# ssm_k loaded and transposed in two halves of its channels, three stage 1 copies moved from VectorE to ScalarE, and the last copies of two stages halved

## The chip, the cores and the metric

The kernel runs on one core of one Trainium2 chip. The metric is the device time of one execution in microseconds (us), the lower the better; a kernel's figure is the median of its runs. "Same" means within 2%. Even fast runs of one kernel on one chip differ by up to 2.9 us here (224.88 to 227.79 us, at mean granted TensorE clocks of 0.999 and 0.985 of full speed), so stages are compared by the trace and not by the total alone.

## The reference, cut to what matters

```python
x = A_q                                            # 1 x 2048 x 512, bf16
# kv = (4-tap causal filter of k with shift_k) * v, per channel
kv_f = rfft(pad(kv));  kf_f = rfft(pad(ssm_k))     # ssm_k: 512 channels x 2048 times
y = irfft(kv_f * kf_f)[:2048] + kv * ssm_D         # long convolution, per channel
h = x + layernorm(x) * y
out = h + relu(layernorm(h) @ w1) @ w2
```

The long convolution is done with matmuls: a transform of ssm_k in two stages, the same for kv, a product, and two inverse stages. Then comes the MLP. ssm_k is stored with time as the last axis, but the first stage needs channels and coarse time on the rows; so the kernel transposes it on TensorE as soon as it is loaded.

## The kernel before

ssm_k is loaded at once (2 MB) as `sk` with 128 partitions, 4 channel blocks and 2048 times. Each of 64 transposes takes every 64th time of all four blocks: 128 weight columns (4 blocks x 32 times), 64 elements apart in memory. Eight share a PSUM bank, which VectorE or ScalarE then copies out.

```python
sk = early.tile([P, DC, S], BF16, name="sk")
nc.sync.dma_start(out=sk[:], in_=A_ssm_k.rearrange("(c p) t -> p c t", p=P))
...
def to_rows(src, q, fl, eng):
    pst = psum.tile([P, 8, P], BF16, tag="ps", name="pst")
    for i in range(8):
        nc.tensor.transpose(out=pst[:, i, :], in_=src[:, :, :, 8 * q + i], identity=ident[:])
    copy(eng, fl[:, :, :, 8 * q:8 * q + 8], pst[:].rearrange("p i (d g) -> p g d i", d=2))
...
skv = sk[:].rearrange("p c (a b) -> p c a b", b=64)
for q in range(8):
    to_rows(skv, q, kfl, "DADADADA"[q])
...
taps(0)                       # 4 matmuls of 512 columns: the filter of k
for gb in range(7):
    group_k(gb)               # stage 1 of ssm_k: 64 loads and 64 matmuls in 0.6 us, 4 copies
    taps(2 * gb + 1)
    taps(2 * gb + 2)
taps(15)
group_k(7)
# then xfl: 64 transposes of kv; the spectrum stage; the product stage, whose end is
#   finish(): psy -> kf   copy("AD"[s] if kp >= 14 else "A", kf[:, s, :, ...], psy)
# then inverse stage 1, b = 0..31 (psi -> bp); the second inverse (pz) needs all of bp
    if b < 31:
        copy("ADAADAAD"[b % 8], dst, ps[:])
    else:
        copy("A", dst[:, 0], ps[:, 0])
        copy("D", dst[:, 1], ps[:, 1])
    ...
    if b in (19, 22, 25, 28):
        row_stats(mv1, (b - 19) // 3)      # VectorE
```

## Time and profile before

| what | before |
|---|---|
| time, median of 3 | 223.93 us (223.79 to 223.94) |
| span of the profiled run | 221.4 us, clock 0.999 |
| sk released | 9.73 us |
| the 64 transposes of sk | 9.73 to 16.07 |
| first stage 1 group, with one tap done | 17.16 |
| transposes of kv start (xfl) | 37.48 |
| product starts | 66.82 |
| inverse stage 1 starts | 98.44 |
| second inverse starts | 114.97 |

The last seven rows are read from the chain of waits and from TensorE's timeline. TensorE is in 85% of that chain, so one can take the kernel as a row of stages on TensorE and ask of each part of the change whether its stage begins or ends sooner. The view of one tile tells how a group of instructions repeats. For `sk` of the kernel before (columns: line, engine, operation, count, shortest/median/longest duration in ns, first and last start in us, shapes):

```profile
L203 PEld LDWEIGHTS <-sk x64: 167/190/212, 9.7 to 15.7; 128*128 128x128 bf16 x64
L203 PE MATMUL pst<-ident,sk x64: 224/258/349, 9.7 to 15.8; 128*128 128x128 bf16 x64
```

The duration of one (258 ns) is not its cost, since they are pipelined. The cost is the distance of starts: (15.8 - 9.7) / 63 = 97 ns on average, cold start included. ("Cold" is the slow clock with which the array begins: in this trace the starts are about 107 ns apart until 12.8 us, and about 88 ns after it, when the array is "warm". The clock column of the views shows 1.00 in both parts.)

### The profile page before, as it was taken

What the parts mean: (1) busy time and instruction counts of PE and PEld (TensorE: products, weight loads), DVE (VectorE), ACT (ScalarE), POOL (GpSimd) and SP (SyncE); (2) the same over time, 40 slices, a digit from 0 to 9 for tenths busy, and PEclk for the clock granted to TensorE, in tenths of its full rate; (3) what the DMA queues carried; (4) which work ended last, traced back from release to release, by engine and by line L of the source; (5) the groups of instructions that cost most, each with busy time, mean ns of one, the idle gap of its engine ahead of it and who ended that gap; (6) DMA issues with size and microseconds to landing.
All of it is one profiled execution on the core that took longest, in us unless ns stands there. A gap on an engine that the chain in (4) does not pass through costs nothing.

```text
span 221.4 us, 7288 instructions
## 1 busy us (share of the span) xinstructions
PE 201.6 (91%) x3111; PEld 140.1 (63%) x3111; DVE 150.3 (68%) x299; ACT 133.0 (60%) x252; POOL 72.0 (33%) x103
## 2 busy tenths in 40 slices
PE   0299799999989999989989899999999999999993
PEld 0294446999978999969977578544444444444452
DVE  4898788889997999966878779761973257130031
ACT  2868877888885888867983889103650066206500
POOL 8399940000008999978400120220022002000000
PEclk9999999999999999999999999999999999999999
DMA  5999920000000000019990000152113110421012
GB/s 178 311 223 204 193 53 4 0 4 6 3 3 3 1 0 0 4 47 238 258 340 14 3 3 3 24 82 58 31 28 80 42 48 4 95 56 42 0 43 54
DMA packets 30384, 15.41 MB, mean 70 GB/s; under 512 B 25520, under 2 KB 29072, under 8 KB 30224
## 3 DMA queue, kind: packets, MB, share of 16 engines
q1 hardware_dynamic: 29520, 14.76, 29.0%
q8 instruction: 24, 0.39, 0.7%
q10 hardware_dynamic: 832, 0.20, 0.4%
q14 instruction: 8, 0.07, 0.1%
HBM read 7.08 MB, written 2.10 MB: 41 GB/s over the span
## 4 chain that ended last, share of the span: by engine, by line
PE 85%; ACT 5%; DMA 4%; DVE 2%; issue 1%; SPq 0%; DVEq 0%; ACTq 0%
PE ps2m L536 18%; PE ps1m L524 16%; PE pz L450 8%; PE psy L343 7%; PE psi L417 7%; PE pkv L262 6%; PE pst L203 6%; PE ps L221 4%; PE ps2k L236 4%; DMA sk<-in_A_ssm_k_dram 4%; PE ps2k L238 3%; PE u L236 3%; PE u L238 3%; ACT ecore L131 1%; ACT zt L461 1%
## 5 line engine op out<-in xcount | busy, mean ns | idle before, releaser
L526 ACT ACTIVATE h1T<-ps1m 128x512 bf16<-128x512 f32 (+3 forms) x55 | 27.4, 514 | 21.2 <-PE ps1m L524 20.3
L524 PE MATMUL ps1m<-hlnT,w 128*128 128x512 bf16 (+3 forms) x220 | 39.6, 336 | 0.3
L536 PE MATMUL ps2m<-w,h1T 128*128 128x512 bf16 (+3 forms) x187 | 39.8, 367 | 0.0
L538 DVE TENSOR_TENSOR o<-ps2m,xh 128x512 bf16<-128x512 f32 (+1 forms) x17 | 11.1, 659 | 37.6 <-PE ps2m L536 32.2
L524 PEld LDWEIGHTS <-w 128*128 128x128 bf16 (+1 forms) x220 | 21.7, 100 | 17.6 <-issue 1.4
L536 PEld LDWEIGHTS <-h1T 128*128 128x128 bf16 (+1 forms) x187 | 17.6, 98 | 21.2 <-issue 3.1
L333 DVE TENSOR_TENSOR t<-u,kf 128x704 fp32r<-128x704 f32 x32 | 26.7, 883 | 3.0 <-ACT usb L329 2.8
L333 POOL TENSOR_TENSOR t<-usb,kf 128x320 fp32r<-128x320 f32 x32 | 28.2, 935 | 1.4 <-ACT usb L329 1.0
L461 ACT CAST zt<-pz 128x512 bf16<-128x512 f32 x16 | 8.4, 593 | 29.5 <-PE pz L450 29.5
L450 PE MATMUL pz<-bp,ecore 32*32 32x128 f32 x1024 | 23.1, 384 | 1.7 <-DVE bp L210 0.9
L470 POOL TENSOR_SCALAR rstd<-mv 128x4 f32<-128x4 f32 (+1 forms) x7 | 1.6, 232 | 70.1 <-DVE mv L477 70.1
L208 ACT CAST a<-ps 128x512 fp32r<-128x512 f32 (+1 forms) x38 | 19.3, 568 | 4.3 <-PE ps L221 4.3
L450 PEld LDWEIGHTS pz<-bp,ecore 32*32 32x32 f32 x1024 | 14.4, 103 | 9.1 <-issue 5.0
L210 DVE CAST a<-ps 128x512 fp32r<-128x512 f32 (+1 forms) x30 | 18.5, 651 | 2.2 <-PE ps L221 2.1
L208 ACT CAST kf<-psy 128x512 fp32r<-128x512 f32 x30 | 17.4, 641 | 1.8 <-PE psy L343 0.3
L475 DVE BATCH_NORM_STATS2 st<-xh 128x6 f32<-128x512 bf16 x28 | 17.3, 678 | 0.0
L262 PE MATMUL pkv<-kT,wdiag 128*128 128x512 bf16 x64 | 15.4, 380 | 1.2 <-issue 1.2
L417 PE MATMUL psi<-dre,kf 128*128 128x256 f32 x64 | 15.5, 284 | 0.9 <-DVE kf L210 0.9
L343 PE MATMUL psy<-t,ipos 128*128 128x512 f32 x48 | 15.9, 391 | 0.0
L417 PE MATMUL psi<-dim,kf 128*128 128x256 f32 x64 | 15.4, 283 | 0.0
L203 PE MATMUL pst<-ident,sk 128*128 128x128 bf16 x64 | 6.3, 277 | 9.7 <-DMA sk<-in_A_ssm_k_dram 9.7
L265 DVE TENSOR_TENSOR vT<-pkv,vT 128x512 bf16<-128x512 f32 x16 | 10.9, 691 | 3.4 <-PE pkv L262 3.4
(113 smaller groups left out, 394.9 us busy)
## 6 DMA issues: line engine op xcount, KB each, us to landing
sk<-in_A_ssm_k_dram SPq DMA_DIRECT2D x1, 2048.0 KB, 8.4
out_dram<-o SPq DMA_DIRECT2D x58, 32.0 KB, 1.6
xh<-in_A_q_dram SPq DMA_DIRECT2D x4, 384.0 KB, 6.8
w<-in_B_w_dram SPq DMA_DIRECT2D x1, 1376.0 KB, 12.8
w<-in_B_w_dram SPq DMA_DIRECT2D x1, 1280.0 KB, 16.2
xh<-in_A_q_dram SPq DMA_DIRECT2D x4, 128.0 KB, 2.8
hlnT<-hln SPq DMA_TRANSPOSE x12, 2.4
w<-in_B_w_dram SPq DMA_DIRECT2D x1, 96.0 KB, 15.9
```

The lines of the kernel that those rows point to most:

```text
L203: nc.tensor.transpose(out=pst[:, i, :], in_=src[:, :, :, 8 * q + i], identity=ident[:])
L208: nc.scalar.copy(out=o, in_=i)
L210: nc.vector.tensor_copy(out=o, in_=i)
L262: nc.tensor.matmul(out=ps[:], lhsT=wdiag[:, rg, j, :], rhs=kT[:, rg, CH * c + 16 - j:CH * c + CH + 16 - j], start=(j == 0), stop=(j == KS ...
L333: eng.tensor_tensor(out=t[:, :, j, :], in0=in0.unsqueeze(1).to_broadcast([P, 2, n, 2]), in1=kfr[:, :, j, ks], op=ALU.mult)
L343: nc.tensor.matmul(out=psy[:], lhsT=m_[:], rhs=t_.rearrange("p j k -> p (j k)"), start=first, stop=not first)
L417: nc.tensor.matmul(out=ps[:, i, :], lhsT=kf[:, c, 4 * m:4 * m + 4, :].rearrange("p r k -> p (r k)"), rhs=d[:].rearrange("p a b -> p (a b)" ...
L450: nc.tensor.matmul(out=pz[32 * a:32 * a + 32, r4, l4, :], lhsT=ecore[rows, rho, n2, :], rhs=rhs, start=(rho == 0), stop=(rho == 1), tile_p ...
L475: nc.vector.bn_stats(out=st[:, t % 4, :], in_=xh[:, t, :])
L524: nc.tensor.matmul(out=ps1[:fsz, :], lhsT=w1[:, c, fc * P:fc * P + fsz], rhs=hlnTs[sc][:, c, part], start=(c == 0), stop=(c == DC - 1))
L526: nc.scalar.activation(out=h1s[sc][:fsz, fc, part], in_=ps1[:fsz, :], func=ACT.Relu)
L536: nc.tensor.matmul(out=ps2[:], lhsT=h1s[sc][:ksz, fc, i * P:(i + 1) * P], rhs=w2[:ksz, fc, ds], start=(fc == 0), stop=(fc == NFC - 1))
```

## The change

Its intent: let TensorE begin when half of ssm_k is there, so that the 9.7 us wait shrinks; even out VectorE and ScalarE in the spectrum stage; and shorten the last copies on which the next stage waits.

```diff
-    nc.sync.dma_start(out=sk[:], in_=A_ssm_k.rearrange("(c p) t -> p c t", p=P))
+    for h in range(2):
+        nc.sync.dma_start(out=sk[:, 2 * h:2 * h + 2, :],
+                          in_=A_ssm_k[2 * h * P:(2 * h + 2) * P, :].rearrange("(c p) t -> p c t", p=P))
...
-    for q in range(8):
-        to_rows(skv, q, kfl, "DADADADA"[q])
+    psts = [psum.tile([P, 8, P], BF16, tag="ps", name="pst") for _ in range(8)]
+    for h in range(2):
+        hs = slice(64 * h, 64 * h + 64)
+        for q in range(8):
+            for i in range(8):
+                nc.tensor.transpose(out=psts[q][hs, i, :], in_=skv[:, 2 * h:2 * h + 2, :, 8 * q + i],
+                                    identity=ident[:], tile_position=(0, 64 * h))
+            if h == 1:
+                rows_out(psts[q], q, kfl, "DADADADA"[q])
...                                     # taps: two ahead of the first group, two after each
-        stage1(gb, xfl, ..., "ADAD", 2 if gb == 7 else 1)
+        stage1(gb, xfl, ..., "ADADADAA" if gb < 7 else "ADAD", 2 if gb == 7 else 1)
...                                     # finish(): the copy of psy to kf
-            copy("AD"[s] if kp >= 16 - LAG else "A", kf[...], psy[...])
+            if kp < 15:
+                copy("AD"[s] if kp >= 16 - LAG else "A", dst, src)
+            else:
+                copy("A", dst[:, 0:136], src[:, 0:136])
+                copy("D", dst[:, 136:256], src[:, 136:256])
...                                     # inverse stage 1
-        if b < 31:
+        if b < 30:
```

A transpose of half the channels has 64 weight columns in place of 128 and fills 64 PSUM partitions: a column tile of the array, at column 0 for the first half and 64 for the second.

More of the change, by code (lines that the diff above doesn't have):

```diff
@@ L197, with rows_out @@
             nc.gpsimd.tensor_copy(out=dtab[:], in_=d0[:].rearrange("p r (o g) -> p o r g", g=8))
-    def to_rows(src, q, fl, eng):
-        pst = psum.tile([P, 8, P], BF16, tag="ps", name="pst")
-        for i in range(8):
-            nc.tensor.transpose(out=pst[:, i, :], in_=src[:, :, :, 8 * q + i], identity=ident[:])
+    def rows_out(pst, q, fl, eng):
         copy(eng, fl[:, :, :, 8 * q:8 * q + 8], pst[:].rearrange("p i (d g) -> p g d i", d=2))
@@ L271 @@
     taps(0)
-    for gb in range(7):
+    taps(1)
+    for gb in range(8):
         group_k(gb)
-        taps(2 * gb + 1)
-        taps(2 * gb + 2)
-    taps(15)
-    group_k(7)
+        for u in range(2 * gb + 2, min(2 * gb + 4, 16)):
+            taps(u)
     for pq in halves:
@@ L285 @@
     for q in range(8):
-        to_rows(kvv, q, xfl, "ADADADAD"[q])
+        pst = psum.tile([P, 8, P], BF16, tag="ps", name="pst")
+        for i in range(8):
+            nc.tensor.transpose(out=pst[:, i, :], in_=kvv[:, :, :, 8 * q + i], identity=ident[:])
+        rows_out(pst, q, xfl, "ADADADAD"[q])
     pl.pop("early")
@@ L303 @@
         spectrum_k(2 * gb + 1)
-        stage1(gb, xfl, lambda o, j, n: a1x[:, o, :, j:j + n], "ADAD", 2 if gb == 7 else 1)
+        stage1(gb, xfl, lambda o, j, n: a1x[:, o, :, j:j + n], "ADADADAA" if gb < 7 else "ADAD", 2 if gb == 7 else 1)
     pl.pop("psF")
@@ L344, in finish @@
                                  start=first, stop=not first)
-            copy("AD"[s] if kp >= 16 - LAG else "A", kf[:, s, :, 2 * kp:2 * kp + 2],
-                 psy[:].rearrange("p (j k) -> p j k", k=2))
+            dst, src = kf[:, s, :, 2 * kp:2 * kp + 2], psy[:].rearrange("p (j k) -> p j k", k=2)
+            if kp < 15:
[3 more added lines that the diff above has]
+                copy("D", dst[:, 136:256], src[:, 136:256])
     for kp in range(16):
```

## The prediction

> **What bounds the kernel now.** I read the page first (engine shares, then the chain of work that ended last), then the time-ordered chain, and then the timeline at the three places that the diff touches. From the page:
>
> ```profile
> PE 201.6 (91%) x3111; PEld 140.1 (63%) x3111; DVE 150.3 (68%) x299; ACT 133.0 (60%) x252; POOL 72.0 (33%) x103
> ...
> PE 85%; ACT 5%; DMA 4%; DVE 2%; issue 1%; SPq 0%; DVEq 0%; ACTq 0%
> ```
>
> TensorE is 85% of the chain that sets the end. So a change on another engine pays only where TensorE stands still. The waits in TensorE's stream are few: 9.7 us for the load of ssm_k, 1.24 us of "issue", about 1.0 us between stage 1 and the product, 0.9 us before the inverse stage, 0.9 us before the second inverse. Here is the chain at the places that matter:
>
> ```profile
> 1.25 8.44 DMA sk<-in_A_ssm_k_dram
> 9.73 6.34 PE pst L203 x64
> 16.09 1.02 ACT kfl L208
> ...
> 25.24 0.54 PE pkv L262 x2
> 25.77 1.24 issue
> 27.02 1.46 PE pkv L262 x6
> ...
> 97.61 0.70 DVE kf L210
> 98.31 0.14 issue
> 98.44 14.64 PE psi L417 x120
> 113.11 1.36 ACT bp L208 x3
> 114.49 0.44 DVE bp L210
> ```
>
> The columns are start, length, and the engine and line. Everything waits for all of sk (9.73). Then come 64 transposes, the last copy (to 17.11), and stage 1 at 17.16. The 1.24 us gap sits between the second and third matmul of one tap, where no data dependency can begin. I take it for an instruction fetch (below).
>
> **What the Trainium skill says.** (1) "TensorE: Matmul & The Clock Gate", Part 1: a matmul of 128 columns repeats every 106.7 ns while the array is cold (about the first 3.4 us of activity), 55.6 ns warm. The trace agrees about the cold part. These windows show the matmuls on sk (an instruction that overlaps two windows counts in both, about 3 each):
>
> ```profile
> 9.70:10.70 1.00, 0.97 (x9) 0.97 (x10) 1.00 1.28 291
> 10.70:11.70 1.00, 1.00 (x13) 1.00 (x11) 1.00 0.89 190
> 11.70:12.70 1.00, 1.00 (x12) 1.00 (x11) 1.00 1.23 261
> 12.70:13.70 1.00, 1.00 (x14) 1.00 (x13) 1.00 1.23 231
> ```
>
> Nine start in the first 0.97 us (108 ns), about 28 in the first 3 us, later about 11 per us (91 ns). Warm transposes of sk run at 91, not 56, ns; the row of xfl's 64 agrees (5.99 us, 94 ns), while the eight of hln with adjacent columns take 0.61 us in all. So the strided weight load is the limit, not the matmul.
> (2) "TensorEngine Tiling (Array Packing)", Tile-to-Partition Mapping, Restrictions: column tiling disables Fast Weight Load. The new transposes are column tiles of 64. No run yet shows such a load here.
> (3) "Runtime: NRT & Kernel Launch", Instruction fetch mechanics: instructions come in blocks of 256 by the sequencer's own DMA queue. The trace agrees: the page lists 24 packets and 0.39 MB of kind "instruction", and two issue gaps in the inverse stage stand exactly 128 matmul-load pairs apart (119.56 and 122.85). The fetch packet ahead of the 1.24 us gap moved at 24.35, TensorE resumed at 27.02: 2.7 us, while DMA transposes filled the engines.
> (4) "ScalarE: Activation LUTs", What ACT_TABLE_LOAD costs: 186 ns + 0.833 per element. For 512 elements 0.61; measured 0.60 for the last kf copy. So an estimate of 0.41 for 272.
>
> **The change, part by part.**
>
> *(a) ssm_k in halves.* Bytes are equal. In 1 us slices from 2 us on the DMA moved 86, 303, 397, 385 GB/s, so 1.05 MB are through at about 5.7 us. The whole load's last data came at about 8.6, its release at 9.7, 1.1 later; so the first half releases at about 6.9 (estimate), the second still at 9.7. But 64 transposes become 128, each again with 128 moving columns (ident), now with 64 weight columns. Cold costs 107 ns whatever the weights: 6.9 + 3.1 us brings 29 of them, to 10.0. The remaining 99 run at a warm pitch p. The matmul gives at least 56 ns. For the weights: fp32 loads of 128 columns in the psi stage repeat every 120 ns (14.64 us / 120 = 122), so half of that, about 60 to 65 ns, for 64 columns without the fast mode. I take p = 62: 10.0 + 99 x 0.062 = 16.1, against 16.06 before. The early start is therefore eaten by doubling the instructions. Copies: q = 0 complete at about 12.7, DVE then has four at 1.155 apart, to about 17.3; ScalarE the same. TensorE does taps(0) and taps(1) meanwhile (8 x 0.23 = 1.84), until 18.0, then stage 1 begins. Before, it began at 17.16 with one tap done, which equals 17.16 + 0.92 = 18.08. Gain about 0.1; each 4 ns of p is 0.4 us.
>
> *(b) Fetch gaps.* Counting instructions in the two programs, the block border that fell on the third matmul of tap 7 (instruction 702) falls there again, but stage 1's group now follows the tap instead of preceding it. The fetch appears about 128 instructions ahead of the border (packets at instructions about 324 and 568; borders 446 and 702). Before, from 568 to 702 were 1.4 us of work, so the gap was 1.24. Now they hold one group and 1.5 taps, about 1.95 us: a gap of 0.5 to 0.75. The neighbouring borders (446, 958) fall about 2.37 us behind their trigger, 0.03 to 0.3 of gap each. Sum about 0.9 against 1.29 before: gain 0.4.
>
> *(c) Three stage 1 copies from VectorE to ScalarE.* TensorE has no wait from 43.5 to 64.4 and sets the 2.72 us cycle. VectorE waits 0.23 per cycle, ScalarE 0.27. In odd cycles ScalarE gets 0.54 more, lags by 0.27, and regains it in the next. The last group (gb = 7) is unchanged. Worth 0.0.
>
> *(d) Last product copies.* The DVE copy of s = 1 (97.61 to 98.30) becomes 0.41 on ScalarE beside 0.40 on VectorE: psi begins about 0.3 earlier.
>
> *(e) Last two copies of inverse stage 1.* Here I expect a loss. Lines of the timeline:
>
> ```profile
> 112.90 0.66 DVE L210 COPY bp<-psi 128x512 f32<-128x512 f32 x1
> 113.11 1.35 ACT L208 COPY bp<-psi 128x512 f32<-128x512 f32 x3 [0.37 <-PE psi L417]
> 113.48 0.68 DVE L405 BATCH_NORM_STATS2 st<-xh 128x6 f32<-128x512 bf16 x1
> 114.19 0.18 DVE L406 BATCH_NORM_AGGREGATE mv<-st 128x2 f32<-128x6 f32 x1
> 114.49 0.42 DVE L210 COPY bp<-psi 128x256 f32<-128x256 f32 x1
> ```
>
> VectorE runs in order: the row statistics of b = 28 stand before its half copy of b = 31, and that copy ends last. Now the half of b = 30 also stands there, one pitch of 0.37 (four such halves took 1.53 us at 65.14). The second inverse needs all of bp. So it starts 0.37 later relative to psi, though ScalarE is done sooner.
>
> Sum: -0.1 - 0.4 + 0.0 - 0.3 + 0.37 = about -0.4. The terms of (a) are the least certain, and an early release at 6.5 or a pitch of 56 would add 0.4 to 0.6 each. I shade to -1.0: 222.9.
>
> **The rivals.** *R1, the front pays in full.* If the transposes keep well ahead (p near 56, early warm clock), VectorE's own work before (f_lo ends just ahead of the first kfl copy at 11.68) and four copies end at 16.4, stage 1 starts at 16.5 with two taps done: 1.6 us ahead; with a fetch gap gone altogether, 2.8 in all. For it: the chain has sk in it at 3.8%. Against: the cold clock in the windows above. Time: about 221.
> *R2, the doubled transposes cost more than the early load brings.* If a 64-column strided load takes as long as the 128-column one (p = 91), the transposes end at 19.0 and stage 1 begins at 20.9: 2.8 later, about 225.7 with the rest. For it: the weight load was the bound at 91 ns, and the fast mode is lost. Against: 120 ns for 128 plain fp32 columns says cost goes with columns.
> *R3, ScalarE becomes the bound of the spectrum stage.* Its load rises from about 2.45 to 2.7 us per 2.72 us cycle. If copies from PSUM slow, TensorE would wait at the next reuse of a buffer; eight buffers give one whole cycle of slack. I give it 0 to 0.5 us.
>
> **Range and chances.** Front between -2.5 and +1.0, fetch gaps +-0.5, (d) and (e) +-0.3: I put 8 in 10 between 221.2 and 224.2. Over 2% faster means below 219.5, 3.4 us under my central figure and below R1; over 2% slower means above 228.4, beyond R2. So 0.03, 0.95, 0.02.
>
> **What would show it.** Right: a first transposition near 6.9 us, spaced 107 ns for 3 us and 60 to 65 after; last one near 16; stage 1 near 18 with two taps before it; one issue gap of 0.5 to 0.75 in tap 7; no TensorE wait in the spectrum stage; psi 0.3 earlier relative to the last psy; the second inverse still released by VectorE's bp, 1.3 us instead of 0.94 after the last psi. Wrong: a spacing near 91 or 107 throughout, the first transposition not before 9.7, a gap over 1 us, or a bp release by ScalarE.

## The result, and the profile after

The changed kernel takes 227.69 us (median of 4, 227.11 to 227.87) against 223.94 for the kernel before. The ratio is 1.0151, 95% interval 1.0111 to 1.0191: slower, but by less than 2%, so "same". A ratio here is the mean time of one kernel's fast runs over that of the other's of the same rounds, so it is not quite the ratio of the medians that are quoted. The prediction (222.9, range 221.2 to 224.2) missed on the slow side.

Busy time and the chain's shares, from the page of the changed kernel:

```profile
PE 207.4 (92%) x3156; PEld 147.1 (65%) x3175; DVE 149.6 (66%) x298; ACT 133.9 (59%) x256; POOL 71.7 (32%) x103
...
PE 73%; DVE 14%; DMA 3%; ACT 2%; issue 2%; POOL 2%; SPq 1%; DVEq 0%; ACTq 0%
```

TensorE is busy 5.8 us more for the same mathematics. VectorE's 14% of the chain should not be read as a new bound. In the second inverse and the row norms the walk back followed VectorE; in the trace of the same kernel's second run (`after_again`) it followed TensorE, with 86% for TensorE and 4% for VectorE. The chain in order of time, changed kernel (start, length, what):

```profile
1.25 5.65 DMA sk<-in_A_ssm_k_dram
6.95 13.94 PE pst L248 x128
20.88 0.54 PE pkv L268 x2
21.48 1.25 PE pkv L268 x5
22.72 0.61 PE ps L220 x64
...
40.73 5.91 PE pst L293 x64
...
100.49 0.44 ACT kf L207
100.95 0.42 DVE kf L209
101.41 7.95 PE psi L429 x64
...
118.10 3.18 PE pz L462 x131
121.28 0.73 issue
122.01 2.57 PE pz L462 x112
```

The transposes begin 2.8 us sooner (6.95) and end 4.8 us later (20.88 against 16.07). They take 13.94 / 128 = 109 ns each, and not only while the clock is cold. The windows on `sk` (matmuls and loads in each stretch; those that lie across a border count twice):

```profile
8.00:9.00 1.00, 1.00 (x12) 1.00 (x11) 1.00 1.01 418
...
16.00:17.00 1.00, 1.00 (x12) 1.00 (x11) 1.00 2.05 166
...
19.00:20.00 1.00, 1.00 (x12) 1.00 (x11) 1.00 0.97 217
```

Twelve less the three carried over is nine per us, at 8 us as at 19 us. (Only between 13 and 15 us, where the first column tile gives way to the second, are there 15 and 14.) In the tile view the load itself has grown, though it has half the columns:

```profile
L248 PEld LDWEIGHTS <-sk x128: 185/203/207, 6.9 to 20.5; 128*64 128x64 bf16 x128
L248 PE MATMUL pst<-ident,sk x128: 267/273/372, 6.9 to 20.6; 128*64 128x128 bf16 x128
```

Where the 3.9 us of span went, by the starts of TensorE's stages in the two traces:

| stage starts | before | after | difference |
|---|---|---|---|
| first stage 1 group, counted with two taps done | 18.08 (17.16 + 0.92) | 22.72 | +4.64 |
| transposes of kv | 37.48 | 40.73 | +3.25 |
| product | 66.82 | 69.77 | +2.95 |
| inverse stage 1 | 98.44 | 101.41 | +2.97 |
| second inverse | 114.97 | 118.10 | +3.13 |
| end of the span | 221.4 | 225.3 | +3.9 |

So the front loses 4.6 us, and 1.4 come back up to the kv transposes (the 1.24 us gap among the taps is gone). The spectrum stage gives back 0.3, the two halved copies together cost 0.2, and 0.8 more goes after the start of the second inverse. The views of what TensorE waited for point at that last part. First before, then after (engine, tile and line, then the releaser: us in total, times, longest):

```profile
PE pkv L262 <- issue: 1.2, 1, 1.2
PE pz L450 <- DVE bp L210: 0.9, 1, 0.9
PE pz L450 <- issue: 0.7, 2, 0.5
```

```profile
PE pz L462 <- issue: 2.4, 3, 0.9
PE pz L462 <- DVE bp L209: 1.1, 1, 1.1
```

Two gaps of "issue" have become three longer ones, though that stage was not edited.

### The profile page after: what moved, and what is told of

It reads as the page before. It is cut to its first block, busy times and chain, and to the rows that moved or that the text cites. A ratio compares the mean times of both kernels' runs of the same rounds, so it can differ in the third digit from the quotient of the medians.

```text
span 225.3 us, 7399 instructions
## 1 busy us (share of the span) xinstructions
PE 207.4 (92%) x3156; PEld 147.1 (65%) x3175; DVE 149.6 (66%) x298; ACT 133.9 (59%) x256; POOL 71.7 (32%) x103
## 4 chain that ended last, share of the span: by engine, by line
PE 73%; DVE 14%; DMA 3%; ACT 2%; issue 2%; POOL 2%; SPq 1%; DVEq 0%; ACTq 0%
PE ps2m L548 14%; PE ps1m L536 13%; PE psy L351 7%; PE pst L248 6%; PE pkv L268 5%; PE pz L462 5%; PE ps L220 4%; PE ps2k L235 4%; DVE st L487 4%; PE psi L429 4%; PE ps2k L237 3%; PE u L235 3%; PE u L237 3%; PE pst L293 3%; DMA sk<-in_A_ssm_k_dram 3%
## 5 line engine op out<-in xcount | busy, mean ns | idle before, releaser
L538 ACT ACTIVATE h1T<-ps1m 128x512 bf16<-128x512 f32 (+3 forms) x55 | 27.4, 514 | 21.2 <-PE ps1m L536 20.3
L548 PE MATMUL ps2m<-w,h1T 128*128 128x512 bf16 (+3 forms) x177 | 38.9, 366 | 0.7 <-issue 0.3
L207 ACT CAST a<-ps 128x512 fp32r<-128x512 f32 (+1 forms) x41 | 20.8, 571 | 2.6 <-PE ps L220 2.6
L462 PEld LDWEIGHTS pz<-bp,ecore 32*32 32x32 f32 x1024 | 13.9, 103 | 11.4 <-issue 6.9
L248 PE MATMUL pst<-ident,sk 128*64 128x128 bf16 x128 | 13.9, 287 | 6.9 <-DMA sk<-in_A_ssm_k_dram 6.9
L207 ACT CAST kf<-psy 128x512 fp32r<-128x512 f32 (+1 forms) x31 | 17.7, 628 | 1.8 <-PE psy L351 0.2
L248 PEld LDWEIGHTS <-sk 128*64 128x64 bf16 x128 | 13.8, 203 | 6.9 <-DMA sk<-in_A_ssm_k_dram 6.9
L209 DVE CAST a<-ps 128x512 fp32r<-128x512 f32 (+1 forms) x27 | 16.7, 648 | 2.3 <-PE ps L220 2.2
L429 PE MATMUL psi<-dre,kf 128*128 128x256 f32 x64 | 15.5, 284 | 1.0 <-DVE kf L209 1.0
L429 PE MATMUL psi<-dim,kf 128*128 128x256 f32 x64 | 15.4, 283 | 0.0
L268 PE MATMUL pkv<-kT,wdiag 128*128 128x512 bf16 x56 | 14.6, 381 | 0.5 <-issue 0.2
```

The costliest lines, as they stand in the source:

```text
L207: nc.scalar.copy(out=o, in_=i)
L209: nc.vector.tensor_copy(out=o, in_=i)
L248: nc.tensor.transpose(out=psts[q][hs, i, :], in_=skv[:, 2 * h:2 * h + 2, :, 8 * q + i], identity=ident[:], tile_position=(0, 64 * h))
L268: nc.tensor.matmul(out=ps[:], lhsT=wdiag[:, rg, j, :], rhs=kT[:, rg, CH * c + 16 - j:CH * c + CH + 16 - j], start=(j == 0), stop=(j == KS ...
L429: nc.tensor.matmul(out=ps[:, i, :], lhsT=kf[:, c, 4 * m:4 * m + 4, :].rearrange("p r k -> p (r k)"), rhs=d[:].rearrange("p a b -> p (a b)" ...
L462: nc.tensor.matmul(out=pz[32 * a:32 * a + 32, r4, l4, :], lhsT=ecore[rows, rho, n2, :], rhs=rhs, start=(rho == 0), stop=(rho == 1), tile_p ...
```

## The experiments

My theory: the loss is the front (128 column-tile transposes at 109 ns), and the tail's 0.8 us is instruction fetch, moved by the 128 added instructions. Rivals: the loss is spread over the copies that were moved or halved; or the gaps come from these. For the 109 ns there were two theories: (A) load and matmul of one column tile follow each other and only different tiles overlap; (B) the strided load into one tile is slow by itself. Twelve runs were made, in three groups, each group on one chip: ten new kernels, and two of the kernels once more. Three of them (e5, e9, e10) ran once, so their state is unknown; they are read by their traces.

### The front alone, and the rest alone

`e1_front` is the kernel before plus the two loads and the 128 transposes, with the old tap order:

```diff
-nc.sync.dma_start(out=sk[:], ...)
+for h in range(2): nc.sync.dma_start(out=sk[:, 2 * h:2 * h + 2, :], ...)
-for q in range(8): to_rows(skv, q, kfl, ...)
+(the 128 transposes of the change)
```

> The kernel before with the front changed alone: ssm_k in two loads, 128 transposes of 64 columns; tap order, stage 1 copies and the last copies as before. If the doubled transposes at 109 ns carry the loss, the last transpose ends near 20.9 us and the time is 227 to 228, all of the loss. If the loss is spread over the other parts (ScalarE's three more copies, the halved last copies), this run stays at 225 to 226.

Measured: 227.93 us against 224.57, ratio 1.0176 (1.0131 to 1.0221). The transposes began at 6.50 us and took 13.95. The interval overlaps that of the whole change (1.0111 to 1.0191), so the front alone, with what its 128 added instructions do later, accounts for the whole loss.

`e2_rest` is the changed kernel with the front undone:

```diff
-(two loads, 128 transposes)
+nc.sync.dma_start(out=sk[:], ...)
+(64 transposes of 128 columns)
```

> The changed kernel with ssm_k whole and 64 transposes of 128 columns again; two taps first, the three copies on ScalarE and the halved last copies stay. If the front carries the loss: 223.3 to 224.5, within 0.3% of before. If the other parts carry a share: 225 or more.

Measured: ratio 0.9951 (0.9905 to 0.9997) from its two fast runs, 224.03 and 222.66; the other two (226.37, 226.51) were slow and lift its median to 225.2. The clock of those two, 0.983 and 0.985, is also that of fast runs of e3_alt; but even 225.2 is far from the changed kernel's 227.7, so the rest of the change does not make the loss. With two fast runs, whether it helps is not settled. Between the kv transposes and the end of the spectrum stage TensorE has one 0.4 us fetch gap, and 0.4 us of waiting for ScalarE's kf at the last group, as in the kernel before; so the three moved copies are off the path, as predicted.

### Why 109 ns

`e3_alt` lets the two column tiles take turns:

```diff
-for h in range(2):
-    for q in range(8):
-        for i in range(8): transpose(..., tile_position=(0, 64 * h))
+for q in range(8):
+    for i in range(8):
+        for h in range(2): transpose(..., tile_position=(0, 64 * h))
```

> The changed kernel, but the two column halves of each transpose follow each other (tile at column 0, tile at column 64, and so on), so all 128 wait for both loads (9.8 us). Theory A, load and matmul of one column tile run one after the other and only different tiles overlap: the spacing falls to 55 to 65 ns, the last transpose ends at 17 to 18.5 us, time 224 to 225.5. Theory B, the strided load of 64 columns itself takes 109 ns: spacing stays 109, the end comes at about 23.8 us, time 230 or more.

Measured: 226.31 us against 224.57, ratio 1.0086 (1.0057 to 1.0115). From its timeline (start, length, group, idle time ahead of it):

```profile
10.05 7.99 PE L248 MATMUL pst<-ident,sk 128*64 128x128 bf16 x127 [3.18 <-DMA sk<-in_A_ssm_k_dram]
```

7.99 / 127 = 63 ns. One transpose had run at 6.5 us, after the first load. The time is above the 224 to 225.5 us expected under A. So half of the 109 ns vanishes when neighbours use different tiles. That fits A, but also a B in which two slow loads can go on side by side; B as it was put (109 ns here too) fails.

`e5_contig` keeps one tile for 64 transposes in a row, but takes 64 neighbouring times as weight columns. It transposes the wrong elements, and the comparison with the reference still passed; so that comparison cannot vouch for the ssm_k term of any run here.

```diff
-in_=skv[:, 2 * h:2 * h + 2, :, 8 * q + i]
+in_=sk[:, 2 * h + q // 4, 64 * (8 * (q % 4) + i):64 * (8 * (q % 4) + i) + 64]
```

> The changed kernel with the 64 weight columns of each of the 128 transposes taken side by side from memory in place of every 64th element (the result is wrong on purpose). If the stride makes the load slow: the spacing falls from 109 to about 60 to 85 ns. If load and matmul of one column tile simply follow each other[...]: it stays at 105 to 110 ns and the time within 1 us of the changed kernel.

```profile
L248 PEld LDWEIGHTS <-sk x128: 106/110/177, 6.9 to 15.1; 128*64 128x64 bf16 x128
...
8.00:9.00 1.00, 1.00 (x12) 1.00 (x11) 1.00 0.96 390
...
12.00:13.00 1.00, 1.00 (x22) 1.00 (x20) 1.00 1.28 268
```

The load takes 110 ns in place of 203. Once the clock is warm the spacing is about 56 ns (22 less the four carried over, in 1 us); the first 3 us, at about 107, are the cold clock. Theory A falls: it forecast 105 to 110 ns here, in one and the same tile. It is the stride. With it gone the transposes end at 15.4 us in place of 20.9. The single time was 224.26 us. Not all of the early end was gained, since TensorE then waited 1.1 us for the k transpose by DMA.

`e9_mm128` and `e10_mm64` make plain matmuls of the strided weights, with 128 and with 64 moving columns (wrong too):

```diff
-nc.tensor.transpose(out=psts[q][hs, i, :], in_=<strided>, identity=ident[:], ...)
+nc.tensor.matmul(out=<fp32, n columns>, lhsT=<strided>, rhs=ident[:, 0:n], ...)   # n = 128, n = 64
```

> The changed kernel with each of the 128 transposes as a plain matmul of the same strided 64-column weights and 128 moving columns, fp32 result (the numbers are wrong on purpose). A control for the next: if it is the load and not transpose mode that sets the spacing, 109 ns stays.

> The same with only 64 moving columns. If the strided load fills the 109 ns by itself: the spacing stays at 105 to 110 ns. If load and matmul of a tile follow each other: it falls by the 27 ns of 64 columns, to about 82.

The tile views, n = 128 and then n = 64:

```profile
L248 PE MATMUL pst<-ident,sk x128: 268/273/373, 6.6 to 20.3; 128*64 128x128 bf16 x128
```

```profile
L248 PE MATMUL pst<-ident,sk x128: 294/297/320, 6.8 to 20.4; 128*64 128x64 bf16 x128
```

(20.3 - 6.6) / 127 = 108 ns and (20.4 - 6.8) / 127 = 107 ns. But this pair alone does not show that halving the matmul takes nothing off, since the array of e10 was still cold at the end. The 512-column matmuls of the taps that follow, in the changed kernel and then in e10:

```profile
L268 PE MATMUL pkv<-kT,wdiag x7: 379/380/390, 20.8 to 22.3; 128*128 128x512 bf16 x7
L268 PE MATMUL pkv<-kT,wdiag x7: 380/607/634, 20.6 to 23.2; 128*128 128x512 bf16 x7
```

So half the columns, on the slow clock, saved little time against e9. What settles it is the changed kernel itself, whose array is cold until about 11 us and warm after it (`sk` in 7:10.8 and in 12:20):

```profile
L248 PE MATMUL pst<-ident,sk x35: 315/316/372, 6.9 to 10.8; 128*64 128x128 bf16 x35
L248 PE MATMUL pst<-ident,sk x79: 273/273/323, 11.7 to 19.9; 128*64 128x128 bf16 x79
```

The matmul gets shorter, the load stays at 203 ns and the starts stay 109 to 110 ns apart (but for the change of tile). Cold, 128 columns (here) and 64 (e10) have the same spacing; and so have 128 columns cold and warm. So B: a load of 64 columns, 64 elements apart, into one column tile occupies it for 107 to 110 ns whatever the matmul is, and loads into two tiles go on side by side (63 ns each). Times were 227.55 and 227.92, one run each. The whole-array load of 128 such columns costs about 88 to 91 ns on a warm array (e6_early below: (15.5 - 9.8) / 63 = 90), less than one half-width load. How the array reads such columns inside was not tested.

### The halved copies

`e7_halves` is the kernel before with only the halved copies of the change; `e4_banks` halves the same copies, but gives each half a PSUM bank of its own and moves the last row statistics behind the loop:

```diff
 # e7_halves: as in the change; one tile psy / ps, halves copied by "A" and by "D"
 # e4_banks
+for e, (tag, js) in enumerate(((f"psy{s}", slice(0, 128)), (f"u{s}", slice(128, 256)))):
+    psy = psum.tile([P, 256], F32, tag=tag)      # kp == 15: matmuls and copies by halves
...
+if b >= 30: pss[1] = psum.tile([P, 2 * P], F32, tag="ps")
-if b in (19, 22, 25, 28):
+if b in (19, 22, 25):
     row_stats(mv1, (b - 19) // 3)
+row_stats(mv1, 3)                                # after the loop
```

> The kernel before with the last product copies and the last two inverse copies halved as in the change, both halves of each in one PSUM bank. Bank theory: VectorE's half waits for ScalarE's, psi starts no earlier (within 0.1 us, against 0.3 earlier with a bank each), and the second inverse's wait for VectorE's bp copy grows from 0.94 to 1.0 to 1.3 us. Time 223.9 to 224.6. If halves in one bank run side by side: psi 0.3 earlier.

> The kernel before with the last product copies and the last two inverse copies halved, each half in a PSUM bank of its own, and the row statistics of the fourth row moved behind the last inverse copy. If the halves of the changed kernel gained nothing because VectorE waits for ScalarE on the shared bank (0.27 us wait for ScalarE's copy in its trace) and because the row statistics stand ahead: psi starts 0.3 us earlier and the second inverse 0.4 us earlier, time 223.1 to 223.4. If halving is useless in itself: 223.9.

The chain at the end of the product in e7_halves, then ScalarE and VectorE in e4_banks at the same place (two lines from two engines' timelines):

```profile
98.64 0.44 ACT kf L208
99.11 0.42 DVE kf L210
99.57 7.96 PE psi L421 x64
```

```profile
98.32 0.86 ACT L208 CAST kf<-psh 128x256 fp32r<-128x256 f32 x2
98.61 0.85 DVE L210 CAST kf<-psh 128x256 fp32r<-128x256 f32 x2
```

In one bank the halves are copied one after the other (0.44, then 0.42), as in the changed kernel (100.49, then 100.95). VectorE's timeline says why: in both kernels it idles 0.27 us before its first half, until ScalarE's kf copy ends. In two banks they run together. TensorE's wait ahead of inverse stage 1 was 0.9 us before, 1.0 in the changed kernel and in e7_halves, and 0.6 in e4_banks. Its wait for VectorE's bp was 0.9, 1.1, 1.0 and 0.6 in the same order. Times: e7_halves 225.35 us against 225.62, ratio 0.9975 (0.9911 to 1.0038), no difference. e4_banks 223.33 against 224.57, ratio 0.9936 (0.9901 to 0.9971). All four e4_banks runs had the full clock (1.0); three of the seven runs of before had it too, at 223.99 to 224.61. So part of that ratio may be the clock. The 0.3 us at each of the two waits is read from the trace. e4_banks also cuts the last matmuls of the product in halves and moves row statistics off VectorE's path to the second wait; what these add was not separated from the banks.

### The fetch gaps

`e6_early` is the kernel before with 64 idle matmuls at the start, while TensorE waits for ssm_k anyway. They add 128 instructions to its stream, as many as the change does.

```diff
+for i in range(64):
+    nc.tensor.matmul(out=pre[:], lhsT=ident[:], rhs=<ident, 224 columns>, start=True, stop=True)
 for q in range(8):
     to_rows(skv, q, kfl, "DADADADA"[q])
```

> The kernel before with 64 idle matmuls of 224 columns on the identity put first on TensorE, where it waits for ssm_k anyway. They add the same 128 instructions as the change's doubled transposes and keep the array warm. Fetch theory: in the second inverse there are three issue gaps of 0.7 to 1.1 us (2.4 to 2.9 in all, as in the changed kernel) in place of two with 0.7 to 1.0 in all. If the gaps come from something else in the change they stay at two. The 64 transposes of ssm_k take 6.0 us in place of 6.3 to 6.8. Time within 1 us of before.

Its chain at the second inverse:

```profile
115.45 3.18 PE pz L454 x131
118.64 1.51 issue
120.15 2.82 PE pz L454 x116
122.97 0.73 issue
123.70 2.71 PE pz L454 x116
126.41 0.86 issue
```

Three gaps, 3.1 us in all, with no other part of the change. Over all traces:

| 128 instructions added | issue gaps of pz |
|---|---|
| no: before, e2, e4, e7, e8 (twice) | 2 each; 0.7, 0.9, 1.0, 1.6, 1.3, 1.6 us in all |
| yes: after (twice), e1, e3, e5, e6, e9, e10 | 3 each; 2.4, 3.3, 2.9, 2.4, 2.8, 3.1, 2.1, 2.4 us in all |

From the start of the second inverse to the end of the span the six traces without them take 106.3 to 107.3 us, the eight with them 107.2 to 108.5. So the tail's gaps belong to where the block borders fall and not to the copies. e6_early itself took 225.75 us against 225.62, ratio 0.9979 (0.9914 to 1.0044). Its transposes were faster, 5.96 us in all with a warm array. In its trace that was spent on a 2.3 us gap among the stage 1 groups.

### A combined version, and the changed kernel again

`e8_best` is e2_rest with the bank-separate halves of e4_banks. Its diff is the two shown.

> A version meant to beat both: ssm_k whole and 64 whole transposes, two taps first and three copies on ScalarE as in the change, halves in a bank each and the row statistics moved as in e4_banks. If the gains add up: 0.7 to 1.1% faster than before, 222 to 223.

Measured: 223.97 us against 225.62, ratio 0.9914 (0.9854 to 0.9973). In the third group it ran again, beside the changed kernel:

> The combined version once more, beside the changed kernel: 0.5 to 1.1% faster than before, 2 to 2.5% faster than the changed kernel.

> The changed kernel on the chip of the last run below, for a comparison on one chip: 1.3 to 1.8% slower than before, three issue gaps of 2.4 to 3 us in all in the second inverse.

This time e8 took 225.74 us against 225.72, ratio 1.0004 (0.9953 to 1.0056), and only 0.7% less than the changed kernel: a miss on both counts. Its profiled run there had clock 0.982 and a 2.3 us fetch gap in stage 1, where the first had 1.0 and 1.3. So it is ahead of the changed kernel in the one group that had both, but that it beats the kernel before is not shown. The changed kernel took 227.29, ratio 1.0080 (1.0033 to 1.0126), with 3.3 us of gaps in the second inverse. Slower again, but by less than the 1.3% expected; the runs of before in this group spread from 224.02 to 226.14.

## Why the prediction was wrong

- *The step that failed* is in (a): "so half of that, about 60 to 65 ns, for 64 columns without the fast mode. I take p = 62". The warm pitch was 109 ns. I scaled the pitch of fp32 loads with the number of columns and left the stride out: the columns of those fp32 loads are side by side, and their matmuls have 256 moving columns, so it was not even shown that the load set the 120 ns. Yet my own comparison of sk with hln (strided against adjacent) had shown the stride to be the limit. With p = 109 my own sum gives 10.0 + 99 x 0.109 = 20.8 us for the last transpose; measured 20.88. It is this one term. The other terms of (a) held: release at about 6.9 (6.95), about 107 ns in the first 3 us (109 to 118, which the load would have set in any case), and that the doubling eats the early start. Where I saw a gain of 0.1 us, stage 1 began 4.6 us later.
- *R2 was the right rival, but too mild.* It assumed at most the 91 ns of the full-width load and dismissed even that with the fp32 loads. A half-width strided load costs more than the full-width one. (Its time was also too low by its own terms: 223.93 + 2.8 and the rest, -0.33, make 226.4, and 225.7 only if the shading of the central figure is taken over too.)
- *(b) was right as to the cause, wrong in its size and place.* I expected 0.9 us of gaps left among the taps. There were none of note: the fetch packet moved at 26.5 us and TensorE came to the third matmul of tap 7 only at 29.5, about 3 us of work and not 1.95. Why the fetch began that much ahead was not tested. And I left the second inverse out: the same border shift made its two gaps three (e6_early), and 0.8 us of span came after that stage's start. That is a missing term of the sum.
- *(c) held*: no new wait of TensorE in the spectrum stage (the 0.4 us for ScalarE's kf at its last group stands in both traces).
- *(d) failed too*: predicted 0.3 us gained, measured none (66.82 to 98.44 before, 69.77 to 101.41 after). I took the two halves to run side by side; in one bank VectorE waits for ScalarE. With a bank each, e4_banks shows the 0.3.
- *(e) had the direction and the releaser right, and was too large*: VectorE's bp copy still releases, the wait grew by 0.13 us (0.94 to 1.07), not 0.37. In the kernel before, VectorE's half started at 114.49, just after ScalarE's half ended at 114.46, so it was held by the bank already and not by the row statistics alone.
- The chances were right in class (within 2%), but the direction was wrong, and the class owes its truth to its width and not to the argument; the range was too narrow on the slow side, since R2 lay outside it.

## What to carry to other kernels

Splitting a load so that compute may start early pays only if the pieces cost no more than the whole: price the smaller instruction with the same access pattern, from a row of the same kind, before counting on the overlap. Halving a copy over two engines gained here only where the halves lay in different PSUM banks. And added instructions on TensorE move its fetch borders for the rest of the program, so compare the issue gaps of later stages too before blaming another part of an edit.

## What the Trainium skill lacked or had wrong

- "TensorE: Matmul & The Clock Gate", LDWEIGHTS: it gives the load time by the number of columns alone, and no time for strided columns. (That an SBUF access which goes to another 16-byte line pays is stated in "SBUF — State Buffer", Specifications, without a figure for weight loads.) Here 64 bf16 columns 64 elements apart repeated every 109 ns in one column tile, the same number side by side every 56 ns (warm); two tiles in turn 63 ns; 128 strided columns over the whole array 88 to 91 ns (warm).
- "Runtime: NRT & Kernel Launch", Instruction fetch mechanics: it calls the crossing of a block border mostly hidden. By number that holds (24 fetch packets in the kernel before, and three gaps of 0.2 to 1.2 us); what it lacks is the price of those that show. Here one cost up to 1.5 us in the second inverse and up to 2.3 us in stage 1, while 256 instructions of the second inverse run in 2.7 to 2.8 us and a fetch packet is followed by TensorE's resuming 2.3 to 2.7 us later (before: 24.3 to 27.02, 117.1 to 119.56; after: 119.6 to 122.01).
- "PSUM — Partial Sum Buffer", Terms: it says that no two engines may access one bank in the same partitions at once. In the traces the halves in one bank do follow each other, by a wait. What it lacks is the price: a copy of 512 columns halved over two engines in one bank took 0.44 and then 0.42 us.
